# One kernel for attention and two mixtures of experts: attention units in pairs, first-mixture blocks of 256 tokens, and three weights at another start in SBUF

## The chip, the cores and the metric

The kernel runs on one core of a Trainium2 chip. The metric is device time in microseconds (us) of one execution. Before the change, three timed runs gave 1914.37, 1915.16 and 1915.44 us (median 1915.16).

## The reference, cut to what matters

Three stages follow one another; the output of one is the input of the next.

```python
def attention(r, k, v, w, u):             # each (4, 8, 768, 48), u (8, 48)
    for t in range(768):                  # per batch and head, state is 48 x 48
        y[t]  = r[t] @ (state + outer(u * k[t], v[t]))
        state = w[t][:, None] * state + outer(k[t], v[t])

def first_mixture(x, w1, w2, w3, w_out):  # x (3072, 384), w1, w2 (384, 1024)
    return ((x @ w1) * (x @ w2)) @ w3 @ w_out

def second_mixture(x, w_gate, w1, w2):    # 8 experts, w1[e] (384, 1024), w2[e] (1024, 384)
    P = exp(logits - logits.max()),  logits = x @ w_gate
    for _ in range(8):                    # Sinkhorn
        P /= P.sum(1); P /= P.sum(0); P *= N / E
    return sum(P[:, e:e+1] * (relu(x @ w1[e]) @ w2[e]) for e in range(8))
```

## The kernel before, in words

**Stages.** The program has three parts. The first (to about 131 us) is written out by hand in a list, `START`: it loads and splits the weights of the first mixture, multiplies w3 by w_out into one weight W34 (384 columns), runs attention units 0 to 6 and starts the first mixture. The second (131 to 437 us) is the loop over slots at line 800, which weaves attention units 7 to 23 and the rest of the first mixture together. The third (437 us to the end) is the second mixture, with expert weights streamed in, TensorE products `zp` (256 columns) and `yp` (384 columns), and the Sinkhorn steps in between. The change rewrites the second part; of the first and third the order of work stays almost as it was.

**Attention.** A unit is 128 tokens of one batch, all heads. For each unit, VectorE runs two scans over the decay w (`scan_f` line 277, `scan_g` line 281) and makes scaled K and R (`ks`, `rp`); GpSimd makes `rk`, the cross factors `kx` and `rx`, and the diagonal term `ec`. TensorE then has small products of 64 by 64: `sc` (K against R, line 325), `trn` (a transpose of K), `yt1` (masked scores times v, into the PSUM tiles `yt`), `up` (K times v, the state's increment) and `yt2` (R times the state, added into `yt`). VectorE folds `up` into the state in eight instructions a unit (`sn_`, line 378), and ScalarE copies `yt` into the block's `xraw`.

**First mixture.** Tokens go through in 8 blocks of 384 (`BLK`), three units each. `x_high` and `x_low` split x into two parts for TensorE (`xhl`); each weight is split the same way (W1 into `w1h`, `w1l` and so on), and a product takes three matmuls: high by high, high by low, low by high. For each of 8 slices f of the hidden width, `pa` (x by W1) and `pb` (x by W2) take 9 matmuls each; ScalarE moves `pa` out (`asb`), VectorE multiplies (`gs`), ScalarE and GpSimd split the product (`gh`, `gl`). `moe_x2` (line 507) takes g by W34 into `po`, 72 matmuls a block. So a block has 8 x 2 x 9 + 72 = 216 matmuls whose moving side is as wide as the block. `moe_log` (line 528) makes the logits of a group of tokens: step 0 multiplies by the gate (`pl`) and VectorE copies that to `lt`; step 1 transposes `lt` on TensorE (`plt`) and VectorE copies that to `L`. One group is one block.

**What sets the order.** Each engine runs its instructions in the order the program issues them. In the loop, four slots make a unit: phase 0 queues the next unit's preparation in `aux`, of which one or two steps are taken in each slot; phase 1 issues `yt2` of the unit before, then `sc` and `trn`; phase 2 issues `yt1`, `up` and the state; phase 3 issues `yt2` once in three units. A slot further carries one `pa`/`pb` pair or a quarter of `po`, by the table `slices`; `logs` places the two steps of the logits one slot apart; the pre-sums of x for the second mixture (`x2s`, `pre_x`) come from the lists `PLACES` and `LASTPLACES`. A stretch in which TensorE leaves the wide matmuls for the small products and comes back is called a visit below.

Of the kernel before, what the change touches and what calls it, by code (L numbers as in the profile page):

```python
# [22 lines left out]
LAG = 3  # L23
LOG0 = 1
S0 = 28
# [36 lines left out]
def tile_rwkv_moe_sinkhorn_moe(  # L62
# [21 lines left out]
    P = 128  # L84
# [6 lines left out]
    BLK = 384  # L91
    UB = BLK // P
    NB = NT // BLK
# [4 lines left out]
    T = 256  # L98
# [19 lines left out]
    mask = const.tile([P, DP], F32, name="mask")  # L118
    eye = const.tile([P, DP], F32, name="eye")
# [5 lines left out]
    lt = const.tile([GP * UB, P], F32, name="lt")  # L125
    nc.vector.memset(gate, 0.0)
    L = const.tile([P, NTT, E], F32, name="L")

# [25 lines left out]

# [17 lines left out]
    w34l = moe.tile([P, NF, DM], F32R, name="w34l")  # L172
    wo = moe.tile([P, NF, DM], F32, tag="gh", name="wo")
# [119 lines left out]
    def ks(n):  # L293
        st[n]["K"] = t = att.tile([P, 34 * 32], F32, tag="K", bufs=1, name="Kt")
        gv = st[n]["G"][:, 1:529].rearrange("p (c b s) -> p b c s", b=2, s=33)[:, :, :, 1:33]
        (nc.gpsimd if n in KS_POOL else nc.vector).tensor_tensor(diag(t), nat["k", n % 2].rearrange("p (a b s) -> p b a s", b=2, s=32), gv, op=ALU.mult)

    def rp(n):
        st[n]["R"] = t = att.tile([P, 34 * 32], F32, tag="R", bufs=2, name="Rt")
        (nc.gpsimd if n in RP_POOL else nc.vector).tensor_tensor(off(t)[:, ::-1], nat["r", n % 2].rearrange("p (a b s) -> p b a s", b=2, s=32),  # L300
                                tot(n)[:, :, :, 0:32], op=ALU.mult)

    def kx(n):
        t = st[n]["K"]
        for g, m_ in enumerate((st[n]["M"][:, 1, :], tot(n)[:, 1, :, 32])):
            nc.gpsimd.tensor_tensor(off(t)[:, g], diag(t)[:, 1 - g], m_.unsqueeze(2).to_broadcast([P, 8, 32]),
                                    op=ALU.mult)

    def rx(n):
        t = st[n]["R"]  # L310
        for g, m_ in enumerate((st[n]["M"][:, 0, :], tot(n)[:, 0, :, 32])):
            nc.gpsimd.tensor_tensor(diag(t)[:, g], off(t)[:, 1 - g], m_.unsqueeze(2).to_broadcast([P, 8, 32]),
                                    op=ALU.mult)
# [11 lines left out]
    def sc(n):  # L325
        Rt, Kt = st[n]["R"], st[n]["K"]
        st[n]["sc"] = s_ = [psa.tile([P, NP, DP], F32, tag=f"sc{h}", name=f"sc{h}") for h in range(2)]
        for p in range(NP):
            for c in range(2):
                for h in range(2):  # L330
                    cs = slice((4 * p + 2 * c) * 32, (4 * p + 2 * c + 2) * 32)
                    mm(s_[h][64 * c:64 * c + 64, p, :], Kt[64 * h:64 * h + 64, cs], Rt[64 * h:64 * h + 64, cs],
                       True, True, pos=(64 * h, 64 * c))

    def trn(n):
        if n - 1 in st:
# [18 lines left out]
    def yt1(n):  # L355
        d = st[n]
        A, vt = d["A"], nat["v", n % 2].rearrange("p (h d) -> p h d", d=DP)
        d["yp"] = yp = [psa.tile([P, NP, DP], F32, tag=f"yt{c}", name=f"yt{c}") for c in range(2)]
        for p in range(NP):
            for h in range(2):  # L360
                for c in range(2):
                    rs = slice(64 * c, 64 * c + 64)
                    o = 64 * (h if c else 1 - h)
                    mm(yp[c][o:o + 64, p, :], vt[rs, 2 * p + h, :], A[rs, h, p, :],
                       p == 0, n % UPB == 0 and c == 0 and p == NP - 1, pos=(64 * c, o))

    def up_(n):
        d = st[n]
        vt = nat["v", n % 2].rearrange("p (h d) -> p h d", d=DP)
        d["up"] = up = [psa.tile([P, NP, DP], F32, tag=f"sc{c}", name=f"up{c}") for c in range(2)]  # L370
        for p in range(NP):
            for h in range(2):
                for c in range(2):
                    rs = slice(64 * c, 64 * c + 64)
                    mm(up[c][64 * h:64 * h + 64, p, :], d["kn"][rs, p, 64 * h:64 * h + 64], vt[rs, 2 * p + h, :],
                       True, True, pos=(64 * c, 64 * h))

    def sn_(n):
# [3 lines left out]
        for c in range(2):  # L382
            sn = att.tile([P, NP, DP], F32, tag="S", bufs=3, name="Sn")
# [12 lines left out]
    def yt2(n):  # L396
        yp, ss, Rt = st[n]["yp"], st[n]["ss"], st[n]["R"]
        for p in range(NP):
            for h in range(2):
                for c in (1, 0):  # L400
# [4 lines left out]
                    cs = slice((16 + 4 * p + 2 * c) * 32, (18 + 4 * p + 2 * c) * 32)  # L405
                    mm(yp[c][o:o + 64, p, :], ss[c][rs, p, :], Rt[rs, cs], False, p == NP - 1, pos=(64 * h, o))

    def xraw(n):
        yp = st.pop(n)["yp"]
        blk, q = n // UB, n % UB  # L410
        if q == 0:
            xr[blk] = moe.tile([P, NP, BLK], F32, tag="xraw", name="xraw")
        xt = xr[blk]
        nc.scalar.activation(xt[:, :, q * P + 64:q * P + 128], yp[1], AF.Copy)
        for h in range(2):
            nc.scalar.activation(xt[64 * h:64 * h + 64, :, q * P:q * P + 64], yp[0][64 - 64 * h:128 - 64 * h], AF.Copy)

    def xd_(n):
        blk, q = n // UB, n % UB
        xt = xr[blk]  # L420
        if blk == NB - 1 or q == UB - 1:
            ts_ = slice(q * P, (q + 1) * P) if blk == NB - 1 else slice(0, BLK)
            for j in range(KD):
                for h in range(2):
                    nc.sync.dma_start(xt[64 * h + D:64 * h + 64, j, ts_],
                                      xt[64 * h + DQ * j:64 * h + DQ * (j + 1), NP - 1, ts_])

    def stage_a0(n):
        rk(n)
        aux.extend([lambda f=f: f(n) for f in (scan_f, scan_g, small, ks, rp, kx, rx)] + [lambda: (cc(n), ec(n))])  # L430

    def each(n, *fs):
        for f in fs:
            f(n)
# [3 lines left out]
    def x_high(blk, q=None):  # L438
        xt = xr[blk]
        if blk not in xs:  # L440
            xhl = moe.tile([P, 2, KD, BLK], F32R, tag="xhl", name="xhl")
            xs[blk] = (xhl[:, 0], xhl[:, 1])
        xh, xl = xs[blk]
        ts_ = slice(0, BLK) if q is None else slice(q * P, (q + 1) * P)
        nc.scalar.activation(xh[:, :, ts_], xt[:, 0:KD, ts_], AF.Copy)

    def x_low(blk, q=None):
        xt = xr[blk]
        xh, xl = xs[blk]
        ts_ = slice(0, BLK) if q is None else slice(q * P, (q + 1) * P)  # L450
        nc.vector.tensor_tensor(xl[:, :, ts_], xt[:, 0:KD, ts_], xh[:, :, ts_].bitcast(F32), op=ALU.subtract)
# [5 lines left out]
    def ab(blk, f, nm, wh, wl):  # L457
        xh, xl = xs[blk]
        m_t[nm, blk, f] = pt = ps.tile([P, BLK], F32, tag={"pa": "mA", "pb": "mB"}[nm], bufs=2, name=nm)
# [800 lines left out]
```

## Time and profile before

| quantity | value |
|---|---|
| timed runs | 1914.37, 1915.16, 1915.44 us |
| the profiled execution | 1915.92 us, span 1914.2 us |
| TensorE busy in the span | 1888.8 us (99%) |
| VectorE, ScalarE, GpSimd busy | 1378.7 us (72%), 686.2 us (36%), 650.0 us (34%) |
| granted TensorE clock | 1.00 |

Read it so: TensorE is busy from about 131 us on without a break, so a change is worth what it takes off or adds to TensorE's own stream, including waits that it opens there. The other engines matter only through the waits they cause. Busy times of TensorE count a matmul longer than the distance to the next one, since matmuls overlap; the distance from start to start is the cost.

### The profile page before, as it was taken

How to read it: one execution, taken by the hardware profiler on the slowest of the kernel's cores; microseconds unless marked ns; L12 is line 12 of the kernel's file. 1: busy time of each engine (PE TensorE's matmuls, PEld its weight loads, DVE VectorE, ACT ScalarE, POOL GpSimd, SP SyncE). 2: the span in 40 equal slices, each digit the busy share in tenths (PEclk: the TensorE clock that was granted, in tenths of full speed). 3: DMA queues.
4: the chain of work that ended last, by engine and by line, in shares of the span. 5: the costliest groups of instructions: out<-in, count | busy, mean ns of one | idle time of the engine just before them, and what ended most of it. 6: DMA issues, size and time to landing. Idle time of an engine off the chain costs nothing.

```text
span 1914.2 us, 38103 instructions
## 1 busy us (share of the span) xinstructions
PE 1888.8 (99%) x15499; PEld 1842.9 (96%) x15499; DVE 1378.7 (72%) x2409; ACT 686.2 (36%) x1322; POOL 650.0 (34%) x867
## 2 busy tenths in 40 slices
PE   6999999999999999999999999999999999999999
PEld 3799999999999999999999999999999999999999
DVE  8866777765887887676767677667677777667666
ACT  6733333344333333333333333333333333333322
POOL 6766666635431313122222222222323231322200
PEclk9999999999999999999999999999999999999999
DMA  9622444346655555555555555555555555555463
GB/s 379 230 87 91 140 134 140 105 148 239 235 184 191 190 196 197 182 199 183 202 188 197 185 200 187 193 176 208 175 200 185 197 194 193 191 182 188 173 204 121
DMA packets 90494, 353.76 MB, mean 185 GB/s; under 512 B 10384, under 2 KB 34256, under 8 KB 64592
## 3 DMA queue, kind: packets, MB, share of 16 engines
q1 hardware_dynamic: 90320, 351.34, 53.1%
q8 instruction: 122, 2.00, 0.4%
q14 instruction: 52, 0.43, 0.1%
HBM read 329.67 MB, written 20.45 MB: 183 GB/s over the span
## 4 chain that ended last, share of the span: by engine, by line
PE 94%; DMA 2%; DVE 2%; ACT 1%; issue 0%; SPq 0%; DVEq 0%; ACTq 0%
PE yp L114 41%; PE zp L114 34%; PE po L114 5%; PE pa L114 5%; PE pb L114 5%; DMA raw<-in_moe_w_dram 1%; PE yt L114 1%; PE w34ps L114 1%; PE trn L114 1%; DMA nat_kn<-in_kn_dram 1%; PE sc L114 1%; PE up L114 0%; PE pl L114 0%; DVE cvp L229 0%; DVE Sn L388 0%
## 5 line engine op out<-in xcount | busy, mean ns | idle before, releaser
L114 PE MATMUL zp<-xc,w1c 128*128 128x256 f32 x5760 | 793.7, 277 | 1.0 <-DVE ct L915 0.6
L114 PEld LDWEIGHTS zp<-xc,w1c 128*128 128x128 f32 x5760 | 766.7, 188 | 4.8 <-ACT ct L922 1.3
L114 PE MATMUL yp<-w2h,hl 128*128 128x384 f32 x1536 | 515.0, 335 | 0.6 <-DVE hl L912 0.6
L114 PE MATMUL yp<-w2l,hh 128*128 128x384 f32 x1536 | 514.6, 335 | 0.0
L114 PE MATMUL yp<-w2h,hh 128*128 128x384 f32 x1536 | 513.1, 334 | 0.0
L907 ACT ACTIVATE hh<-ct 128x512 fp32r<-128x512 f32 x384 | 236.8, 632 | 526.3 <-DVE ct L915 265.8
L915 DVE TENSOR_TENSOR ct<-ct,zp 128x512 f32<-128x512 f32 x576 | 377.3, 681 | 47.0 <-PE zp L114 41.4
L620 POOL TENSOR_TENSOR w1c<-w1s,w1c 128x512 fp32r<-128x512 f32 (+1 forms) x120 | 127.6, 1064 | 779.9 <-ACT w1c L616 779.9
L922 ACT ACTIVATE ct<-zp 128x512 f32<-128x512 f32 x256 | 153.6, 600 | 440.8 <-PE zp L114 440.8
L114 PEld LDWEIGHTS yp<-w2h,hl 128*128 128x128 f32 x1536 | 288.3, 188 | 1.0 <-DVE hl L912 0.9
L114 PEld LDWEIGHTS yp<-w2h,hh 128*128 128x128 f32 x1536 | 288.4, 188 | 0.2 <-issue 0.2
L114 PEld LDWEIGHTS yp<-w2l,hh 128*128 128x128 f32 x1536 | 288.4, 188 | 0.0
L1087 DVE SCALAR_TENSOR_TENSOR acc<-yp,Pm,acc 128x384 f32<-128x384 f32 x336 | 205.8, 613 | 103.9 <-PE yp L114 103.8
L912 DVE SCALAR_TENSOR_TENSOR hl<-ct,hh 128x512 fp32r<-128x512 f32 x384 | 276.5, 734 | 0.0
L918 DVE TENSOR_TENSOR ct<-ct,zp 128x512 f32<-128x512 f32 x128 | 87.9, 687 | 162.8 <-PE zp L114 162.8
L918 DVE TENSOR_TENSOR ct<-zp,ct 128x512 f32<-128x512 f32 x128 | 88.3, 690 | 74.6 <-ACT ct L922 62.7
L620 POOL TENSOR_TENSOR w1c<-w1raw,w1c 128x128 fp32r<-128x128 f32 (+1 forms) x90 | 56.7, 630 | 195.3 <-ACT w1c L616 195.3
L612 POOL TENSOR_TENSOR w1s<-w1raw 128x128 f32<-128x128 f32 x240 | 120.8, 524 | 0.2
L487 POOL TENSOR_TENSOR gl<-gs,gh 128x384 fp32r<-128x384 f32 x64 | 75.4, 1179 | 104.0 <-ACT gh L483 101.2
L114 PE MATMUL pa<-xhl,w1h 128*128 128x384 f32 x384 | 100.4, 342 | 1.5 <-ACT w34s L255 1.5
L114 PE MATMUL pb<-xhl,w2h 128*128 128x384 f32 x384 | 98.1, 336 | 0.4 <-DVE cv L230 0.4
L478 DVE TENSOR_TENSOR gs<-pb,asb 128x384 f32<-128x384 f32 x64 | 35.4, 553 | 66.6 <-PE pb L114 48.1
(130 smaller groups left out, 1908.6 us busy)
## 6 DMA issues: line engine op xcount, KB each, us to landing
xc<-xd SPq DMA_DIRECT2D x192, 1024.0 KB, 4.9
xc<-xd SPq DMA_DIRECT2D x64, 768.0 KB, 4.3
xd<-x2s SPq DMA_DIRECT2D x53, 256.0 KB, 2.7
w1raw<-in_e_w_dram SPq DMA_DIRECT2D x32, 384.0 KB, 3.1
w2raw<-in_e_w_dram SPq DMA_DIRECT2D x32, 384.0 KB, 3.1
raw<-in_moe_w_dram SPq DMA_DIRECT2D x8, 1024.0 KB, 9.5
nat_w<-in_w_dram SPq DMA_DIRECT2D x24, 264.5 KB, 3.4
nat_k<-in_kt_dram SPq DMA_DIRECT2D x24, 256.0 KB, 4.0
```

Source lines behind the costliest of these rows:

```text
L114: nc.tensor.matmul(o, lhsT, rhs, start=start, stop=stop, **kw)
L478: nc.vector.tensor_tensor(t, m_t.pop(("pb", blk, f)), m_t.pop(("asb", blk, f)), op=ALU.mult)
L487: nc.gpsimd.tensor_tensor(gl[:, f, :], m_t.pop(("gs", blk, f)), gh[:, f, :].bitcast(F32), op=ALU.subtract)
L612: eng.tensor_tensor(tmp_[:, many.index(r), :], at_(a), at_(b), op=ALU.add if sg == 1 else ALU.subtract)
L620: eng.tensor_tensor(lo[:, d0:d1, :], sv, hi[:, d0:d1, :].bitcast(F32), op=ALU.subtract)
L907: nc.scalar.activation(hh, src, AF.Relu)
L912: nc.vector.scalar_tensor_tensor(hl, src, 0.0, hh.bitcast(F32), op0=ALU.max, op1=ALU.subtract)
L915: nc.vector.tensor_tensor(o, a, b_, op=ALU.add)
L918: nc.vector.tensor_tensor(o, a, b_, op=ALU.subtract)
L922: nc.scalar.activation(t, src, AF.Copy)
L1087: nc.vector.scalar_tensor_tensor(dst, yp, so["Pm"][:, tt, e:e + 1], dst, op0=ALU.mult, op1=ALU.add)
```

## The change

Five things change, all in the second part of the program.

1. **Blocks.** The first two blocks keep 384 tokens; the other 2304 tokens go in nine blocks of 256 in place of six of 384 (`BLKS`). A group of logits is four tiles of 128 tokens (six groups) in place of three (eight groups).
2. **Pairs.** From unit 7 on, two units go together through `sc`, `trn`, `yt1`, `up`, the state and `yt2`. A chunk c has 24 steps: eight of `po` for block c+1, then 16 of `pa` and `pb` for block c+2. A `turn` before step 0 has `yt2` of the old pair, `sc` and `trn` of the new one; a `middle` before step 9 has `yt1`, `up` and the states of a pair.
3. **A table of times.** `aux`, `slices` and `logs` are replaced by hooks at 24*c + j. The logits stand at steps 8.6 and 9.6 of chunks 0, 1, 3, 5 and 7; the sixth group comes later, in the second mixture.
4. **Buffers.** K and R of a unit live in halves of one tile `krr` with rings of spare places, and from unit 10 on the loads of r, k, w, rn and kn have one buffer each (v keeps two). `pre_group` goes; all pre-sums are `pre_x` pieces, and part of the first expert weights is prepared on GpSimd.
5. **Starts in SBUF.** Small gap tiles are put in so that `w1h`, `w1l`, `w2h`, `w2l`, `w34h` and `w34l` begin at 160 modulo 256 bytes of a partition. Before, all six begin at 96. The moving tiles `xhl`, `gh` and `gl` begin at 96 in both kernels.

```diff
-    BLK = 384
-    NB = NT // BLK
+    T = 256
+    BLKS = [(0, 384), (384, 384)] + [(t, T) for t in range(768, NT, T)]
+    NB = len(BLKS)
+    FU = 6
+    NC = NB - 2
...
+    const.tile([P, 16], F32, name="gap_const")
+    mw.tile([P, 16], F32, name="gap_mw")
     w1h = mw.tile([P, KD, FF], F32R, name="w1h")
...
     w34l = moe.tile([P, NF, DM], F32R, name="w34l")
+    moe.tile([P, 48], F32, name="gap_moe")
...
-    def sc(n):
+    def sc(*us):
+        s_ = pair("sc")
+        for u_, n in enumerate(us):
...
-    def yt1(n):
+    def yt1(*us):
+        yp = pair("yt")
...
-    def up_(n):
+    def up_(*us):
+        up = pair("sc")
...
-    def moe_log(blk, step, pool=None, tag="mA", bufs=2):
+    UL = P // GP
+    def moe_log(grp, step, pool=None, tag="mA", bufs=2):
...
+    def prep(n, base, scale=1.0):
+        def put(d, *fs):
+            event(base + 0.5 + d * scale, *fs)
+        put(0, lambda: rk(n), lambda: scan_f(n))
+        put(1, lambda: scan_g(n))
...
+        put(6, lambda: rx(n))
+        put(8.8, lambda: cc(n))
+        put(9.6, lambda: ec(n))
...
+    def middle(*us):
+        yt1(*us)
+        up_(*us)
+        for n in us:
+            sn_(n)
...
-    for s in range(S0, NSL):
...
+    for k in range(NC):
+        step(k, -0.5, lambda k=k: turn(k, k + 1))
+        step(k, 4.6, lambda k=k: x_high(k + 2))
+        step(k, 5.6, lambda k=k: x_low(k + 2))
+        if k + 1 < NC:
+            step(k, 9 - 0.5, lambda k=k: middle(*units(k + 1)))
+        if k + 2 < NC:
+            n = FU + 2 * k + 4
+            prep(n, 24 * k + 1)
+            prep(n + 1, 24 * k + 12)
...
+    step(0, 8.6, lambda: moe_log(0, 0))
+    step(0, 9.6, lambda: moe_log(0, 1))
+    for g_ in range(1, NTT // UL - 1):
+        step(2 * g_ - 1, 8.6, lambda g_=g_: moe_log(g_, 0))
+        step(2 * g_ - 1, 9.6, lambda g_=g_: moe_log(g_, 1))
...
+    for c in range(-1, NC):
+        for j in range(10 if c < 0 else 0, 24):
+            run(24 * c + j)
+            if j < 8:
+                moe_x2(c + 1, j, 8)
+            else:
+                f = (j - 8) // 2
+                if j % 2 == 0:
+                    pa(c + 2, f)
...
+                else:
+                    pb(c + 2, f)
...
```

The order of instructions shows where the logits stand. First TensorE in the slot loop of the kernel before, at one of the eight groups of logits: the end of a `pb`, the product `pl`, and then a visit; the transpose `plt` comes 46 rows on.

```order
L114 MATMUL pb<-xhl,w2h 128x384 x2
L114 MATMUL pb<-xhl,w2l 128x384
L114 MATMUL pl<-x2s,gate 32x128 x9
L114 MATMUL yt_3642<-Rt,Sn 64x64
L114 MATMUL yt_3641<-Rt,Sn 64x64
```

The transpose itself stands before the next visit's first product:

```order
L114 MATMUL pb<-xhl,w2h 128x384 x2
L114 MATMUL pb<-xhl,w2l 128x384
L114 MATMUL plt<-ident,lt 128x96
L114 MATMUL yt_3887<-ec,nat_v_103 64x64
L114 MATMUL yt_3888<-ec,nat_v_103 64x64
```

So between the two stand a visit and two products `pa`, `pb` of nine wide matmuls each. TensorE after the change, chunk 3: the last two rows of the pair's `up` (its PSUM tiles have the tag `sc`, its left operands are `krr` and `nat_v`), `pl`, one `pb`, `plt`, and the next `pa`.

```order
L113 MATMUL sc_3874<-nat_v_105,krr 64x64
L113 MATMUL sc_3875<-nat_v_105,krr 64x64
L113 MATMUL pl<-x2s,gate 32x128 x12
L113 MATMUL pb<-xhl,w2h 128x256 x2
L113 MATMUL pb<-xhl,w2l 128x256
L113 MATMUL pb<-xhl,w2h 128x256 x2
L113 MATMUL pb<-xhl,w2l 128x256
L113 MATMUL pb<-xhl,w2h 128x256 x2
L113 MATMUL pb<-xhl,w2l 128x256
L113 MATMUL plt<-ident,lt 128x128
L113 MATMUL pa<-xhl,w1h 128x256 x2
L113 MATMUL pa<-xhl,w1l 128x256
```

Now `pl` follows the pair's `up` at once, and only one `pb` of nine stands between `pl` and `plt`. VectorE before, around the copy to `lt` that `plt` needs:

```order
L478 TENSOR_TENSOR gs<-pb,asb 128x384
L283 SCALAR_TENSOR_TENSOR Gt<-nat_w_106,d_63 128x527
L538 COPY lt<-pl 96x128
L350 COPY_PREDICATED ec<-mask,sc_3819 128x256
L350 COPY_PREDICATED ec<-mask,sc_3820 128x256
```

VectorE after, at the same group of chunk 3 (`Sn` with its 64-column pieces is the state; the last four go to a spare place in `nat_n1`):

```order
L766 TENSOR_TENSOR x2s<-x2s 128x256
L509 TENSOR_TENSOR xhl<-xraw,xhl 128x768
L456 SCALAR_TENSOR_TENSOR Sn<-s_more,T_3226,sc_3874 128x64 x4
L456 SCALAR_TENSOR_TENSOR Sn<-Sn,T_3226,sc_3875 128x64 x4
L456 SCALAR_TENSOR_TENSOR Sn<-Sn,T_3486,sc_3874 128x64 x4
L456 SCALAR_TENSOR_TENSOR nat_n_110<-Sn,T_3486,sc_3875 128x64 x4
L598 COPY lt<-pl 128x128
L536 TENSOR_TENSOR gs<-pb,asb 128x256
L602 COPY L<-plt 128x32
```

The copy to `lt` stood behind a scan and ahead of the mask copies; it now stands behind all sixteen instructions of the pair's state.

## Rows read from the trace of the kernel before

**Rows 1.** The page: TensorE's busy time, and the chain's shares by line.

```profile
PE 1888.8 (99%) x15499; PEld 1842.9 (96%) x15499; DVE 1378.7 (72%) x2409; ACT 686.2 (36%) x1322; POOL 650.0 (34%) x867
PE yp L114 41%; PE zp L114 34%; PE po L114 5%; PE pa L114 5%; PE pb L114 5%; DMA raw<-in_moe_w_dram 1%; PE yt L114 1%; PE w34ps L114 1%; PE trn L114 1%; DMA nat_kn<-in_kn_dram 1%; PE sc L114 1%; PE up L114 0%; PE pl L114 0%; DVE cvp L229 0%; DVE Sn L388 0%
```

**Rows 2.** Second part: window, us, busy PE, PEld, DVE, ACT, POOL, clock, DMA, GB/s.

```profile
131.00:437.00 306.00, 306.00 (x3771) 291.86 (x3767) 216.65 (x470) 119.16 (x278) 180.87 (x167) 1.00 0.39 122
```

**Rows 3.** TensorE's timeline at two visits (start us, us, then the group).

```profile
371.98 0.34 PE L114 MATMUL pb<-xhl,w2l 128*128 128x384 f32 x1
372.25 0.86 PE L114 MATMUL pl<-x2s,gate 128*32 128x128 f32 x18
373.04 0.69 PE L114 MATMUL yt<-Rt,Sn 64*64 64x64 f32 x32
...
374.54 0.59 PE L114 MATMUL pa<-xhl,w1h 128*128 128x384 f32 x2
374.98 0.34 PE L114 MATMUL pa<-xhl,w1l 128*128 128x384 f32 x1
...
377.76 0.25 PE L114 MATMUL plt<-ident,lt 96*128 96x96 f32 x1
...
379.02 0.62 PE L114 MATMUL pa<-xhl,w1h 128*128 128x384 f32 x2
379.48 0.35 PE L114 MATMUL pa<-xhl,w1l 128*128 128x384 f32 x1
...
380.72 0.51 PE L114 MATMUL pb<-xhl,w2h 128*128 128x384 f32 x2
...
382.28 0.51 PE L114 MATMUL pa<-xhl,w1h 128*128 128x384 f32 x2
```

**Rows 4.** The same view in the second mixture: 256-wide products in the steady stream.

```profile
543.46 1.53 PE L114 MATMUL zp<-xc,w1c 128*128 128x256 f32 x12
544.82 0.33 PE L114 MATMUL yp<-w2h,hh 128*128 128x384 f32 x1
```

**Rows 5.** The same view where the second mixture begins.

```profile
453.97 0.87 PE L114 MATMUL zp<-xc,w1c 128*128 128x256 f32 x6
454.68 0.34 PE L114 MATMUL po<-gl,w34h 128*128 128x384 f32 x1
```

**Rows 6.** The same view again, the first matmul after a visit.

```profile
203.85 0.62 PE L114 MATMUL pa<-xhl,w1h 128*128 128x384 f32 x2
```

**Rows 7.** VectorE's timeline: the unit's state after that visit, and a scan.

```profile
204.03 1.61 DVE L388 SCALAR_TENSOR_TENSOR Sn<-Sn,T,up 128x64 f32<-128x64 f32 x8
205.57 0.68 DVE L300 TENSOR_TENSOR Rt<-nat_r,Ft 128x512 f32<-128x512 f32 x1
...
212.56 2.09 DVE L279 TENSOR_TENSOR_SCAN Ft<-nat_w,d 128x528 f32<-128x528 f32 x1 [1.23 <-POOL Rt L312]
```

**Rows 8.** VectorE's timeline beside the visits of rows 3.

```profile
370.57 1.25 DVE L279 TENSOR_TENSOR_SCAN Ft<-nat_w,d 128x528 f32<-128x528 f32 x1
...
374.67 0.26 DVE L538 COPY lt<-pl 96x128 f32<-96x128 f32 x1
374.85 0.77 DVE L350 COPY_PREDICATED ec<-mask,sc 128x256 f32<-128x256 uint32 x2
```

**Rows 9.** VectorE's groups from 131 to 437 us (count, busy us, mean ns).

```profile
L283 DVE TENSOR_TENSOR_SCAN Gt<-nat_w,d 128x527 f32<-128x527 f32 x16 | 28.3, 1769 | 0.0
L279 DVE TENSOR_TENSOR_SCAN Ft<-nat_w,d 128x528 f32<-128x528 f32 x15 | 27.0, 1800 | 8.7 <-POOL Rt L312 8.7
...
L699 DVE TENSOR_TENSOR x2s<-x2s 128x256 f32<-128x256 f32 x34 | 24.8, 732 | 0.4
L706 DVE TENSOR_TENSOR x2s<-x2s 128x256 fp32r<-128x256 f32 x38 | 14.1, 419 | 1.1 <-ACT x2s L703 1.1
L350 DVE COPY_PREDICATED ec<-mask,sc 128x256 f32<-128x256 uint32 x34 | 12.9, 433 | 0.0
L296 DVE TENSOR_TENSOR Kt<-nat_k,Gt 128x512 f32<-128x512 f32 x16 | 12.1, 758 | 0.0
```

More of the change, by code (lines that the diff above doesn't have):

```diff
@@ new lines, in ks @@
+        if n < FU + 3:
+            t = krr[:, 0:34 * 32]
+            st[n]["K"] = both(t)
+            eng.tensor_tensor(diag(t), kv, gv, op=ALU.mult)
+            if n == FU + 2:
+                ka_home.extend([both(t)[0], nat["w", 1][:, 0:HALF]])
+                kk_ring.extend([st[n - 1]["kn"].rearrange("p a b -> p (a b)"), both(t)[1], nat_n1[:, 0:HALF]])
+                kk_ring.rotate(-2)
+        else:
+            st[n]["K"] = K = ka_home[n % 2], kk_next()
+            for g in range(2):
+                eng.tensor_tensor(alt(K[g], g), kv[:, g], gv[:, g], op=ALU.mult)
@@ L423, in xd_ @@
+    def xd_(n):
+        blk, q = UBLK[n]
+        xt = xr[blk]
+        if (q + 1) * P == BLKS[blk][1]:
             for j in range(KD):
                 for h in range(2):
[L425 to L434, printed above, removed]
@@ L436, in tile_rwkv_moe_sinkhorn_moe @@
-    xs = {}
[L438 to L442, printed above, removed]
-        xh, xl = xs[blk]
[L444 to L451, printed above, removed]
+                    nc.sync.dma_start(xt[64 * h + D:64 * h + 64, j, :],
+                                      xt[64 * h + DQ * j:64 * h + DQ * (j + 1), NP - 1, :])
@@ L711, in pre_x @@
         return sums, high, low
-    def pre_group(sb, g, tag, tmp_, eng):
-        t = spaced(pools["w"], [P, 2, len(XP_[g][4]), T], F32R, tag, "xpre")
-        sums, high, low = factors(XP_, g, XB, x2[sb], tmp_, t, eng)
-        def end():
-            low()
-            xd[sb, g] = dram.tile(list(t.shape), F32, name=f"xd{sb}{g}")
-            nc.sync.dma_start(xd[sb, g], t.bitcast(F32))
-        return sums, high, end
     def ld_x(n, g):
@@ L776, in tile_rwkv_moe_sinkhorn_moe @@
[L776 to L786 removed]
+        return [lambda i=i: part(i) for i in range(3)]
@@ new lines, in prep @@
+    def prep(n, base, scale=1.0):
[3 more added lines that the diff above has]
+        put(1, lambda: scan_g(n))
+        put(2, lambda: small(n))
+        put(3, lambda: ks(n))
+        put(4, lambda: rp(n))
+        put(5, lambda: kx(n))
+        put(6, lambda: rx(n))
+        put(8.8, lambda: cc(n))
+        put(9.6, lambda: ec(n))
+        for nm, d in (("rn", 2), ("kn", 2), ("w", 4), ("k", 6), ("r", 7)):
+            m = n + (2 if n < ONE - 1 else 1)
+            if m < NU and not n == ONE - 1 - 0:
+                put(d, lambda nm=nm, m=m: load(m, (nm,)))
@@ L787, in tile_rwkv_moe_sinkhorn_moe, with front, front_end @@
+    def front(*us):
+        sc(*us)
+        for n in us:
+            trn(n)
+    def front_end(*us):
+        for n in us:
+            kn_(n)
+        for n in us:
+            cp_(n)
+    def middle(*us):
+        yt1(*us)
+        up_(*us)
+        for n in us:
+            sn_(n)
     tx0 = []
@@ new lines, in tile_rwkv_moe_sinkhorn_moe, with units, turn @@
+    s_more = att.tile([P, NP, DP], F32, name="s_more")
+    def units(k):
+        return tuple(u_ for u_ in (FU + 2 * k, FU + 2 * k + 1) if u_ > FU)
+    def turn(k_old, k_new):
+        old, new = (units(k) if 0 <= k <= NC - 1 else () for k in (k_old, k_new))
+        for n in old:
+            yt2(n)
+        if new:
+            front(*new)
+        if old:
+            xraw(*old)
+            xd_(old[-1])
+        if new:
+            front_end(*new)
+    step(-1, 10 - 0.5, lambda: turn(-1, 0))
@@ new lines, in tile_rwkv_moe_sinkhorn_moe @@
+    for sb_ in range(NS - 1):
+        for m_, r_ in enumerate(ORDER):
+            if sb_ < NS - 2:
+                t_, w_, d_ = 24 * 3 * sb_ + 9.7 + 4.2 * m_, WORK[m_ % 4], (5, 9)
+            elif m_ < 3:
+                t_, w_, d_ = 24 * 3 * sb_ + 9.7 + 4 * m_, WORK[(0, 1, 3)[m_]], (4, 8)
+            else:
+                t_, w_, d_ = 24 * (3 * sb_ + 1) + 1.7 + 1.75 * (m_ - 3), LATE[m_ % 6], (2, 4)
+            place(t_, *d_, lazy(lambda sb_=sb_, r_=r_, w_=w_: pre_x(sb_, r_, w_(), 0, nc.vector)))
@@ new lines, in open_w @@
+    def open_w():
+        st_attn.close()
+        pools["w"] = ctx.enter_context(tc.tile_pool(name="wp", bufs=1, side="right", reuse_waits="tile"))
+        ld_w1(0)
+        ld_w1(1)
+        st_pa.close()
+        pools["z"] = ctx.enter_context(tc.tile_pool(name="psz", bufs=1, space=PSUM, side="right",
+                                                    reuse_waits="tile"))
+        for g in range(2):
+            spaced(pools["w"], [P, 4, T], F32, f"w1c{g}0", "unused")
+            ld_x(0, g)
@@ L1143, in sk_both @@
         sk_rows()
-    for x_ in late:
-        sk.append(lambda x_=x_: moe_log(*x_, pool=pools["y"], tag="col", bufs=1))
+    for t_ in range(2):
+        sk.append(lambda t_=t_: moe_log(NTT // UL - 1, t_, pool=pools["y"], tag="col", bufs=1))
     sk.extend([sk_max0, sk_max1, sk_max2])
```

383 lines of the change are left out of this document (178 added, 205 removed).

## The prediction

> **What bounds the kernel now.** I read the page's busy shares and its chain of waits first. TensorE is busy 99% of the span, and five of its products (`yp`, `zp`, `po`, `pa`, `pb`) hold 90% of the chain [rows 1]. Then the windows: from 131 to 437 us, the part that the change rewrites, TensorE is busy 306.00 us of 306.00 at a granted clock of 1.00, while VectorE is busy 216.65 us (71%), GpSimd 59% and ScalarE 39% [rows 2]. No wait of TensorE is left there to take away. So the change can gain only by making TensorE's stream cheaper, and any wait that it opens is lost in full. The last view is TensorE's timeline, for the distance from one matmul's start to the next; the busy time counts overlaps twice and is no use for that.
>
> **The wide matmuls.** In both kernels the first two blocks have 384 tokens. The other 2304 tokens cost 6 blocks of 216 = 1296 matmuls before, and 9 of 216 = 1944 after. Before, nine matmuls of 384 columns take from 380.72 to 382.28, so 173.3 ns each [rows 3], and 1296 x 173.3 = 224.6 us. A 256-wide product in a like shape exists in the second mixture: twelve `zp` take 543.46 to 544.82, 113.3 ns each [rows 4]. At the start of that mixture six take 453.97 to 454.68, 118.3 ns each [rows 5]. With these, 1944 cost 220.3 us (-4.3) or 230.0 us (+5.4). I take 113.7, near rows 4, because that is how a 256-wide product runs in a steady stream, and the second part is one; the few in rows 5 stand at the end of a long run of 384-wide `po`. That is 221.0 us, a gain of 3.6.
>
> The new starts of the weights I cost at nothing beside this. No row shows what a start is worth: the `zp` of rows 4 and those of rows 5 read the same kind of tiles at the same starts, 160 for the weight and 96 for the moving side, yet differ by 5 ns. If the start decides for `pa`, `pb` and `po`, its worth lies between these two rows, so within the ends already named.
>
> The Trainium skill ("TensorE: Matmul & The Clock Gate", Back-to-back issue gap) gives the gap of an isolated matmul at full clock as its columns over 2.4 ns plus 2.5 ns. By it 384 columns cost 162.5 ns and 256 cost 109.2, and the blocks' sum would go from 210.6 to 212.3 us, 1.7 slower in place of 3.6 faster. Both rows lie above it, by 10.8 and 4.1 ns, so the excess is no constant here, and I go by the rows.
>
> **The visits.** Each time TensorE leaves the wide stream for small products and comes back, it loses something at either edge. Entering: from the start of the last `pb` to `pl` is 371.98 to 372.25, 0.27 in place of 0.173, so 0.10. Leaving: two `pa` take 374.54 to 374.98, 0.44 in place of 0.347, and 379.02 to 379.48, 0.46; so 0.09 and 0.11 [rows 3]. A visit costs about 0.21 us. From 131 us to the first `zp` I count 41 visits in the order before and 19 after: 22 x 0.21 = 4.6 us gained. The small products themselves stay the same in number, and so does the gate's: 8 x 9 small `pl` before, 6 x 12 after.
>
> **The new wait.** `plt` needs the copy of `pl` to `lt`. Before, `pl` starts at 372.25, the copy is over by 374.85 [rows 8], and `plt` comes at 377.76 [rows 3], so 2.9 us are to spare. After, `pl` follows the pair's `up` directly, only one `pb` stands between it and `plt`, and on VectorE the copy stands behind the pair's sixteen state instructions. Call the end of `up` T. A visit ends at 203.85 [rows 6] and the state starts at 204.03; eight of its instructions take until 205.57, 0.193 each [rows 7]. So sixteen run from T + 0.18 to T + 3.26, and with the copy's 0.26 [rows 8] `plt` may start at about T + 3.5. TensorE is there sooner: `pl` has 24 passes at 0.79 / 18 [rows 3] = 1.05, `pb` 9 x 0.1137 = 1.02, with the edge 0.2, so T + 2.3. It waits 1.25 us. Behind `plt` on TensorE stands all that follows, the next `pa` first, so nothing covers it. The group occurs in chunks 0, 1, 3, 5 and 7: 5 x 1.25 = 6.3 us lost. Bounds: nothing, if the state of the first unit starts while the second unit's `up` still runs and the copy is early; 5 x 3 = 15 if VectorE is itself 1.75 us late with the state.
>
> **VectorE's load.** Per pair it has 2 x (1.80 + 1.77 for scans, 0.76 and 0.68 for K and R, 0.76 for mask copies, 1.54 for the state) = 14.6 us [rows 7, 9]. A chunk adds eight `gs` at about 0.42 (the two-input 256-wide sum, 419 ns [rows 9]) = 3.4, `x_low` at about 0.9, and 24 / 4.2 = 5.7 pieces of the second mixture's sums at (24.8 + 14.1) / 38 = 1.02, so 5.8. With a microsecond for small ones that is 26 us. TensorE's chunk is 216 x 0.1137 = 24.6 and 2 x 2.6 of small products (1.50 from 373.04 to 374.54, 1.1 within 377.76 to 379.02 [rows 3]), with edges and gate some 30.8. So VectorE is about 84% busy in chunks 0 to 6, against 71% before, and its work comes in lumps: two scans and a sum can stand ahead of something TensorE wants. Bounds: 0, if each lump lies where TensorE is far from it, and 14 us, by the third rival. I take 2 in all, nearer to 0, because `gs`, `x_low` and the states stand in the table where their inputs become ready.
>
> At nothing I cost the rest: the single buffers for r, k, w, rn and kn (a chunk of 30 us lies between a pair's loads and their use; if that cover goes, a load's few us appear once a unit in a scan's start), the rings for K and R, the copy of whole pairs by ScalarE (39% busy), and GpSimd's share of the expert weights. The second mixture keeps its order; the first `zp` just starts when the second part ends.
>
> **Sum.** 1915.92 - 3.6 - 4.6 + 6.3 + 2 = 1916.0 for an execution like the profiled one. The median of the runs shown lies 0.76 lower, so 1915.3; call it 1915.5.
>
> **Rivals.**
> - B, the waits stay hidden: VectorE starts the states with the first unit's `up`, or `gs` and the copy find it free, and only the two gains are left: 1915.16 - 8.2 = 1907. For it: VectorE still idles a sixth of the chunk. Against it: sixteen instructions in a row are sixteen, and 3.1 us exceed the 2.1 us of `pl` and `pb`.
> - C, VectorE cannot follow in the seven heavy chunks. The trace has the same scan at 1.25 us and at 2.09 [rows 7, 8]; with the pair's factors crowded the long form rules, 4 scans a pair add 4 x 0.3 = 1.2 us to the 26, and a lump of 2 us lies ahead of `x_low`. `x_low` is issued at step 5.6 and the block's first `pa` at step 8, so about 2.4 x 1.02 = 2.4 us later; less its own 0.9, it decides from 1.5 us of backlog on. Then TensorE waits about 2 us a chunk, 7 x 2 = 14 in place of 2: 1927. For it: 84% is an average, and the logits add to it. Against: TensorE's own stalls give VectorE time back.
> - D, what a matmul costs above its columns does not shrink with its width, and the changed starts do not alter that. The 384-wide rows lie 13.3 ns above 160.0, the 256-wide of rows 4 lie 6.6 above 106.7 and those of rows 5 11.6. At 118.3 ns the wide sum is 9.0 more than I took: 1924.5. The Trainium skill's rule above has such a constant, though a smaller one. For it: rows 5 stand right beside `po`, whose neighbours they would be. Against: `zp` in the long stream keeps 113.3. This is also the case in which the new starts do nothing that the change could be after.
>
> **How the numbers follow.** This kernel's runs can tell about 0.2%, 3.8 us, from no change. My forecast A (gains and new waits cancel) has 0.40, with its own range 1911.5 to 1919.5; B 0.29, C 0.18, D 0.13. Nearly all of A lies within 0.2%: 0.34, with 0.03 to either side. So faster 0.32, same 0.34, slower 0.34. The range runs from 1906.5, which holds B but for its low edge, to 1925, which holds D and leaves out the larger half of C: about 0.16 is left out.
>
> **What would show it.** In the changed kernel's trace: 256-wide `pa` and `pb` 113 to 114 ns apart in mid-slot (D: 118 or more); nineteen visits; five idle times of TensorE ahead of `plt`, some 1.2 us each, released by VectorE's `lt` (B: none); idle times ahead of the first `pa` of a block released by `xhl`, few (C: seven of 2 us); and the first `zp` within 2 us of where it is now. I am wrong if TensorE shows waits for loads or for GpSimd's factors ahead of `sc`, which I cost at nothing, or if the second mixture itself changes its length.

## The result, and the profile after

The changed kernel takes 1932.13 us (median of 5 runs, 1931.54 to 1934.70) against 1915.16: a ratio of 1.0092, 95% interval [1.0077, 1.0107], so about 17 us slower. The forecast was no change, and the time lies above its range. The span of the profiled execution is 1933.0 us, 18.8 more than before. The profiled executions of starts_96, plt_late and starts_224 below have `zp` 115.5 ns apart in the second mixture in place of 114.1, some 8 us in all, so of these three only the second part is read.

The window that answers to [rows 2] (same columns) shows where: TensorE had no idle time in it before, and has now.

```profile
131.00:437.00 306.00, 289.60 (x4236) 280.80 (x4228) 227.89 (x485) 108.23 (x271) 171.89 (x184) 0.99 0.36 110
```

TensorE's waits from 131 to 520 us in the changed kernel (who waits, for what; us in total, times, the longest). Before, the same view held only the last two kinds and one `yp` wait of 0.6 us.

```profile
PE plt L113 <- DVE lt L598: 7.2, 5, 2.0
PE pb L113 <- DVE gs L536: 6.2, 8, 1.3
PE pa L113 <- DVE xhl L509: 2.9, 6, 0.6
PE yp L113 <- DVE hl L993: 2.2, 1, 2.2
PE zp L113 <- ACT ct L1003: 1.2, 1, 1.2
PE pl L113 <- issue: 0.7, 1, 0.7
PE zp L113 <- DVE ct L996: 0.6, 1, 0.6
PE zp L113 <- DVE ct L999: 0.3, 1, 0.3
```

All three large ones have VectorE at the other end. The second mixture as a whole did not grow. These rows of the two kernels give the first and last start of its `zp` (min, median and max ns, then the starts in us): it begins 19.6 us later and lasts 1458.4 us where it lasted 1459.7. First before, then after:

```profile
L114 PE MATMUL zp<-xc,w1c x5760: 276/276/387, 437.2 to 1896.9; 128*128 128x256 f32 x199
```

```profile
L113 PE MATMUL zp<-xc,w1c x5760: 276/276/394, 456.8 to 1915.2; 128*128 128x256 f32 x199
```

One part of the 18.8 us is no wait. In chunk 5, behind its longest wait for `plt`, TensorE runs at a granted clock of 0.50 (1.2 GHz) from 345.8 to 349.2 us, and nine `pb` take 1.92 us there, 213 ns each. The windows row first (columns of [rows 2]), then TensorE's timeline:

```profile
346.00:349.00 3.00, 3.00 (x16) 3.00 (x16) 0.40 (x2) 0.38 (x1) 0.43 (x1) 0.50 0.90 244
```

```profile
344.92 0.30 PE L113 MATMUL plt<-ident,lt 128*128 128x128 f32 x1 [1.98 <-DVE lt L598]
...
346.38 0.63 PE L113 MATMUL pb<-xhl,w2h 128*128 128x256 f32 x2
...
348.30 0.63 PE L113 MATMUL pa<-xhl,w1h 128*128 128x256 f32 x2
```

That stretch costs 1.6 us against the usual distance. The kernel before has a granted clock of 1.00 in the whole second part [rows 2]. Of the five timed executions two have a mean clock of 0.999 (1934.70, the profiled one, and 1933.33 us) and three 1.000 (1931.54, 1931.80 and 1932.13), so the median's 17 us stand without such a stretch.

The wait ahead of `plt`, TensorE's timeline in chunk 0, which answers to [rows 3]:

```profile
173.59 0.86 PE L113 MATMUL pl<-x2s,gate 128*32 128x128 f32 x24
174.38 0.50 PE L113 MATMUL pb<-xhl,w2h 128*128 128x256 f32 x2
...
177.23 0.30 PE L113 MATMUL plt<-ident,lt 128*128 128x128 f32 x1 [1.53 <-DVE lt L598]
```

And VectorE beside it, the first and last of the state's four groups, then the copy, which answers to [rows 7, 8]:

```profile
173.73 0.86 DVE L456 SCALAR_TENSOR_TENSOR nat_n<-Sn,T,sc 128x64 f32<-128x64 f32 x4 [7.15 <-PE sc L113]
...
176.04 0.85 DVE L456 SCALAR_TENSOR_TENSOR Sn<-Sn,T,sc 128x64 f32<-128x64 f32 x4
176.80 0.28 DVE L598 COPY lt<-pl 128x128 f32<-128x128 f32 x1
```

`pl` follows `up` at 173.59, so that is T; the state takes 173.73 to 176.89, and `plt` starts at T + 3.6; the forecast had T + 3.5.

The waits for `gs` are the other kind. VectorE in chunk 2, without a gap:

```profile
246.69 1.79 DVE L302 TENSOR_TENSOR_SCAN Ft<-nat_w,d 128x528 f32<-128x528 f32 x1
248.41 1.20 DVE L766 TENSOR_TENSOR x2s<-x2s 128x256 fp32r<-128x256 f32 x1
249.53 0.41 DVE L536 TENSOR_TENSOR gs<-pb,asb 128x256 f32<-128x256 f32 x1
249.87 1.72 DVE L306 TENSOR_TENSOR_SCAN Gt<-nat_w,d 128x527 f32<-128x527 f32 x1
251.50 0.22 DVE L313 RECIPROCAL Mt<-Ft 128x16 f32<-128x16 f32 x1
251.65 0.77 DVE L314 TENSOR_TENSOR T<-Ft 128x8 f32<-128x8 f32 x1
252.34 0.41 DVE L536 TENSOR_TENSOR gs<-pb,asb 128x256 f32<-128x256 f32 x1
```

From `gs` to `gs` is 2.8 us, and TensorE's pair `pa`, `pb` takes 18 x 0.1133 = 2.04. `pb` has two PSUM buffers, so VectorE may be one slot late and not two. Further on in the same lump TensorE stands still:

```profile
254.87 0.28 PE L113 MATMUL pa<-xhl,w1l 128*128 128x256 f32 x1
256.43 0.50 PE L113 MATMUL pb<-xhl,w2h 128*128 128x256 f32 x2 [1.29 <-DVE gs L536]
```

The step from start to start is 1.56 us in place of 0.113: the wait costs 1.45, not the 1.29 that the view calls idle, and the step behind it (0.23 us) is another 0.11 longer than usual.

The distance of the wide products, TensorE's timeline at two places, which answers to [rows 4, 5]. First `pa` and the next `pb` in the middle of a chunk, then a `po` run from its second matmul to the `pa` behind it:

```profile
242.13 0.39 PE L113 MATMUL pa<-xhl,w1h 128*128 128x256 f32 x2
...
243.15 0.39 PE L113 MATMUL pb<-xhl,w2h 128*128 128x256 f32 x2
```

```profile
228.63 0.28 PE L113 MATMUL po<-gl,w34h 128*128 128x256 f32 x1
...
236.99 0.28 PE L113 MATMUL pa<-xhl,w1h 128*128 128x256 f32 x1
```

Nine in 1.02 us are 113.3 ns each; 71 `po` in 8.36 us are 117.7. Nearly every `po` (501 of 568), and under half of `pa` and `pb`, run at the slower distance. Over the 1776 undisturbed 256-wide steps ahead of the first `zp` the mean is 115.9 ns.

### The profile page after: what moved, and what is told of

Its sections match the earlier page's. It is cut to its first block, busy times and chain, and to the rows that moved or that the text cites. A ratio compares the mean times of both kernels' runs of the same rounds, so it can differ in the third digit from the quotient of the medians.

```text
span 1933.0 us, 39529 instructions
## 1 busy us (share of the span) xinstructions
PE 1886.9 (98%) x16145; PEld 1846.2 (96%) x16145; DVE 1401.3 (72%) x2452; ACT 684.2 (35%) x1342; POOL 651.8 (34%) x903
## 4 chain that ended last, share of the span: by engine, by line
PE 75%; DVE 1%; ACT 0%; issue 0%; POOL 0%; DVEq 0%; ACTq 0%
PE yp L113 41%; PE zp L113 34%; PE po L113 0%; DVE ct L996 0%; DVE hl L993 0%; DVE acc L1164 0%; ACT hh L988 0%; ACT ct L1003 0%; ACT gh L541 0%; PE pcs L113 0%; DVE w2l L740 0%; PE pl L113 0%; POOL gl L545 0%; ACT w2h L739 0%; DVE ct L999 0%
## 5 line engine op out<-in xcount | busy, mean ns | idle before, releaser
L545 POOL TENSOR_TENSOR gl<-gs,gh 128x256 fp32r<-128x256 f32 (+1 forms) x88 | 76.0, 869 | 126.4 <-ACT gh L541 126.4
L113 PE MATMUL pb<-xhl,w2h 128*128 128x256 f32 (+1 forms) x528 | 106.3, 296 | 6.7 <-DVE gs L536 6.2
L113 PE MATMUL pa<-xhl,w1h 128*128 128x256 f32 (+1 forms) x528 | 105.9, 293 | 3.7 <-DVE xhl L509 2.9
L113 PEld LDWEIGHTS pb<-xhl,w2h 128*128 128x128 f32 x528 | 83.2, 190 | 10.6 <-DVE gs L536 8.5
```

The lines of the kernel that those rows point to most:

```text
L113: nc.tensor.matmul(o, lhsT, rhs, start=start, stop=stop, **kw)
L545: nc.gpsimd.tensor_tensor(gl[:, f, :], m_t.pop(("gs", blk, f)), gh[:, f, :].bitcast(F32), op=ALU.subtract)
```

## Experiments

Each kernel was timed beside the kernel before on the same chip, and the ratios are to that. Theory W: the time is lost in TensorE's waits for VectorE. Rival S: the 256-wide products are dear, and the new starts decide it. Under W there is a second question, whether VectorE has too much to do (load) or only the wrong thing next (order).

**starts_96.**

```diff
-    const.tile([P, 16], F32, name="gap_const")
...
-    mw.tile([P, 16], F32, name="gap_mw")
     w1h = mw.tile([P, KD, FF], F32R, name="w1h")
...
     w2l = mw.tile([P, KD, FF], F32R, name="w2l")
+    mw.tile([P, 16], F32, name="gap_mw")
...
-    moe.tile([P, 48], F32, name="gap_moe")
+    moe.tile([P, 64], F32, name="gap_moe")
...
-        m2.tile([P, 112], F32, name="gap_m2")
+        m2.tile([P, 128], F32, name="gap_m2")
```

> The changed kernel with w1h, w1l, w2h, w2l, w34h and w34l at 96 modulo 256 again; nothing else moves by a byte. Theory W (the loss is waits that TensorE now has for VectorE, the starts are worth nothing): 1932 us, within 2. Theory S (the 256-wide matmuls are what is dear, and their spacing hangs on the starts): pa and pb leave 113 ns and go to 118 or more throughout, some 1000 matmuls by 5 ns or more, so 1937 us or above; or, if 160 is the worse start, po falls from 118 to 113 ns, 500 by 5 ns, and 1929.5.

Measured: 1935.23 us, ratio 1.0112 [1.0095, 1.0130], between the two forecasts. In its second part 4 of 1788 256-wide steps kept 113 to 115 ns (782 of 1776 in the changed kernel); the mean excess over 113.5 was 6.3 ns (11.3 us in all, against 4.2 in the changed kernel). So S is right that the starts set the distance. But the waits shrank as the products grew, those for `gs` from 6.2 to 3.6 us and those for `xhl` from 2.9 to 1.2, so 7 us of slower products cost only 3, which this pair of runs can't tell from none.

**plt_late.**

```diff
-    step(0, 9.6, lambda: moe_log(0, 1))
+    step(0, 12.6, lambda: moe_log(0, 1))
-        step(2 * g_ - 1, 9.6, lambda g_=g_: moe_log(g_, 1))
+        step(2 * g_ - 1, 12.6, lambda g_=g_: moe_log(g_, 1))
```

> The changed kernel with the transpose plt three steps later (step 12.6 in place of 9.6). Theory W: the five idle times ahead of plt, 7.2 us in the profile, go, and with each some 0.27 us of getting back to speed, so 1923.5 us within 2. Rival V (VectorE is behind anyway, and the time comes back as waits for gs or xhl): 1929 to 1932.

Measured: 1926.10 us, ratio 1.0062 [1.0049, 1.0076]: 6 us less than the changed kernel, and between the two forecasts. TensorE's waits up to 450 us:

```profile
PE pb L113 <- DVE gs L536: 7.1, 9, 1.3
PE pa L113 <- DVE xhl L509: 2.8, 5, 0.9
PE pl L113 <- issue: 1.4, 1, 1.4
```

The kind `plt` is gone; `gs` has taken 0.9 us of it.

**half_scans.**

```diff
-        nc.vector.tensor_tensor_scan(t, src("w", n)[:, 0:528], d1[:, 0:528], 0.0, op0=ALU.mult, op1=ALU.add)
...
+        c_ = 528 if n < FU + 4 else 264
+        nc.vector.tensor_tensor_scan(t[:, 0:c_], src("w", n)[:, 0:c_], d1[:, 0:c_], 0.0, op0=ALU.mult, op1=ALU.add)
...
```

> The changed kernel, but from unit 10 on the two scans cover only half of their columns (the other half keeps what an earlier unit left), so each scan is about 0.8 us shorter; all else stands where it stood. Theory V (VectorE's load delays gs and xhl): the waits for gs (6.2 us) and xhl (2.9 us) shrink to 2 or less in sum and 1921 to 1925 us results, with the waits ahead of plt still there at 5 to 7 us. Rival P (it is the places in the table and not the load): the waits stay and 1931 us or more results.

Measured: 1925.26 us, ratio 1.0051 [1.0038, 1.0064]. Its waits:

```profile
PE plt L113 <- DVE lt L606: 7.5, 5, 2.0
PE pb L113 <- DVE gs L544: 2.5, 3, 1.3
...
PE pa L113 <- DVE xhl L517: 0.6, 1, 0.6
```

The `gs` and `xhl` kinds fell from 9.1 to 3.1 us and `plt` kept its own, near what theory V forecast. So the scans are most of what delays them; shorter scans are less load and smaller lumps at once, and this run does not part the two.

**before_160.** The kernel before with the gaps (mask and eye moved to the pool of the attention to make room).

> The kernel before, with only the starts of the six weights moved from 96 to 160 modulo 256 (mask and eye change pool to make room, the moving tiles stay at 96). Theory W: 1915 us within 2, 384-wide matmuls 173 to 174 ns apart as before. Theory S: their spacing changes by some ns; 1300 matmuls by 5 ns would give 1908.5 or 1921.5.

Measured: 1916.32 us, ratio 1.0007 [0.9998, 1.0015]. The starts alone gain nothing where the products are 384 wide. In its trace these stand 174.9 ns apart on average, against 173.7 before, and the first `zp` comes 1.6 us later; the ratio can't tell that from no change.

**fix_low.** On top of plt_late:

```diff
-        step(k, 5.6, lambda k=k: x_low(k + 2))
+        step(k, 4.9, lambda k=k: x_low(k + 2))
```

> The later plt of plt_late, and x_low issued at step 4.9 in place of 5.6, ahead of the first unit's R on VectorE (its input from ScalarE was there 1.4 us before VectorE came to it). If each wait ahead of a block's first pa is only this order: the waits for xhl (2.8 us, 0.27 more each) go and 1926.1 becomes about 1922. Rival V (VectorE is short of time, the wait comes back at gs): 1925 or more.

Measured: 1922.19 us, ratio 1.0036 [1.0023, 1.0048], as forecast. Waits up to 437 us:

```profile
PE pb L113 <- DVE gs L536: 6.0, 8, 1.3
PE pa L113 <- DVE xhl L509: 0.5, 2, 0.2
```

**fix_g.** On top of fix_low, the second unit's steps behind its first scan come one step later:

```diff
-    def prep(n, base, scale=1.0):
+    def prep(n, base, scale=1.0, more=0):
...
-            event(base + 0.5 + d * scale, *fs)
+            event(base + 0.5 + d * scale + (more if d else 0), *fs)
...
-            prep(n + 1, 24 * k + 12)
+            prep(n + 1, 24 * k + 12, 1.0, 1)
```

> As fix_low, and the second unit's preparation behind its first scan one step later, so that its two scans no longer stand in three steps with the gs of the same slots. If the lump of scans is what delays gs: the waits for gs (7.1 us in nine) shrink to some 3 and about 1918 us results. If the total load delays gs: no change against fix_low, within 1.5 us. A third outcome: the factors come too late for the next pair's sc, slower than fix_low.

Measured: 1915.51 us, ratio 1.0001 [0.9992, 1.0010]. Its one kind of wait up to 437 us, and VectorE at the lump shown above:

```profile
PE pb L113 <- DVE gs L536: 2.7, 3, 1.2
```

```profile
243.24 1.79 DVE L302 TENSOR_TENSOR_SCAN Ft<-nat_w,d 128x528 f32<-128x528 f32 x1
244.96 1.20 DVE L766 TENSOR_TENSOR x2s<-x2s 128x256 fp32r<-128x256 f32 x1
246.08 0.41 DVE L536 TENSOR_TENSOR gs<-pb,asb 128x256 f32<-128x256 f32 x1
246.42 1.72 DVE L306 TENSOR_TENSOR_SCAN Gt<-nat_w,d 128x527 f32<-128x527 f32 x1
248.06 0.39 DVE L536 TENSOR_TENSOR gs<-pb,asb 128x256 f32<-128x256 f32 x1
```

The work is the same, instruction for instruction, and from 131 to 437 us VectorE is busy 234.8 us where it was 235.0 in fix_low; the next `gs` now comes right behind the second scan, 1.98 us after the one before. So order alone can take more than half of these waits away (6.0 to 2.7 us of idle time): 6.7 us less than fix_low, for one step. Some 5 of them remain where the mean clock is alike, 1.000, since fix_low's two such runs took 1920.73 and 1920.86 us and the median of fix_g's eight is 1915.6. The edit also moves K, R and what GpSimd makes of them by the step; what each of these gave was not tested.

**fix_pool.** On top of fix_low:

```diff
-            place(t_, *d_, lazy(lambda sb_=sb_, r_=r_, w_=w_: pre_x(sb_, r_, w_(), 0, nc.vector)))
+            place(t_, *d_, lazy(lambda sb_=sb_, r_=r_, w_=w_, m_=m_: pre_x(sb_, r_, w_(), 0, nc.gpsimd if m_ % 3 == 1 else nc.vector)))
```

> As fix_low, and every third piece of the second mixture's sums (about 2 us a chunk) runs on GpSimd in place of VectorE. If VectorE's load delays gs: the waits for gs shrink to some 3 us and about 1918 us results. Rival: GpSimd's work beside VectorE makes VectorE's scans as much longer, or makes gl late, and it is no faster than fix_low.

Measured: 1924.13 us, ratio 1.0048 [1.0035, 1.0061]; the waits for `gs` are 6.8 us in six, one of 2.5. That is no gain, but it doesn't speak against load, since VectorE's load hardly fell. These are the windows of fix_low and of fix_pool (columns of [rows 2]):

```profile
131.00:437.00 306.00, 299.43 (x4324) 292.06 (x4319) 235.01 (x510) 113.06 (x286) 172.54 (x190) 1.00 0.39 120
```

```profile
131.00:437.00 306.00, 298.21 (x4308) 291.04 (x4307) 232.98 (x477) 112.39 (x283) 201.91 (x218) 0.99 0.39 120
```

The sums that stay on VectorE are 14.7 us less, yet it is busy only 2.0 us less, because much of what stays grew, such as the second scan (1.62 to 1.84 us on average) and R (0.57 to 0.72), beside a GpSimd that is busy 29 us more. This is the rival that the expectation named.

**fix_g_96, moving_160, starts_224.** On top of fix_g, the starts alone: weights back at 96; weights at 160 and the moving tiles at 160 too; weights at 224.

> fix_g with the six weights back at 96 modulo 256, as starts_96 was to the changed kernel. If a start is worth what the spacing in starts_96 showed (every 256-wide product of the second part at about 120 ns, none at 113) and waits had swallowed half of it: 5 to 6 us above fix_g, 1920.5 to 1921.5, with spacings of 118 to 121 throughout. If the starts are worth only the 3 us that starts_96 lost: 1918.5. If that profile was a chance: 1915.5.

> fix_g with the moving tiles of the first mixture (xhl, gh, gl) at 160 modulo 256 too, the weights staying at 160. If what matters is that weight and moving side differ by 64: all 256-wide products at 118 to 120 ns as with both at 96, so 5 us above fix_g, 1920.5. If only the weight's own start matters: 1915.5 and the same mixture of 113 and 118 ns.

> fix_g with the six weights at 224 modulo 256, so 128 from the moving tiles in place of 64. If a larger distance frees po as well, which at a distance of 64 stays at 118 ns in nearly all its 576 products: up to 1181 products by 4.4 ns, 5 us less than fix_g, 1910.5. If any distance other than 0 does the same: 1915.5 and the same mixture of 113 and 118. If 64 is the one good distance: 118 to 121 throughout, as in fix_g_96, 1919 to 1920.

Measured: 1919.16 us, ratio 1.0020 [1.0012, 1.0029]; 1919.95, 1.0022 [1.0013, 1.0031]; and 1927.87, 1.0020 [1.0011, 1.0029] on a chip on which the kernel before took 1923.93. The first two stand clear of fix_g's 1.0001 [0.9992, 1.0010]: 3.7 to 4.4 us, between the forecasts of 3 and of 5 us or more. By its trace fix_g_96 loses 6.8 us on the 256-wide products, gains 0.5 on the 384-wide ones, and 1.7 of the waits that fix_g has left are gone. TensorE's timeline of fix_g_96 in mid-chunk:

```profile
240.58 0.40 PE L113 MATMUL pa<-xhl,w1h 128*128 128x256 f32 x2
...
241.66 0.40 PE L113 MATMUL pb<-xhl,w2h 128*128 128x256 f32 x2
```

Nine take 1.08 us, 120 ns each, and moving_160 has the same 120. So it is no property of 160: with weight and moving side both at 96 or both at 160 at most 4 of 1822 steps keep 113 to 115 ns. Nor is it the chip: fix_k below, at 160 against 96 on the same chip, has 722 of 1812. A distance of 128 was no better than 64, as far as the slower chip lets one say: 263 of its 1820 steps took 112 to 115 ns, the others 116 to 126, which is nearest to the third outcome.

**fix_k.** On top of fix_g, the second unit's K and R one step later still.

> fix_g with the second unit's K and R (and what GpSimd makes of them) another step later, since two of the three waits that fix_g has left (1.2 us each) stand ahead of a gs that VectorE does behind K and a sum. If it is again the order: those two go and 1913 us results. If the load decides, they move to the next gs: 1915 to 1916. If the factors then miss the next pair's sc: slower than fix_g.

Measured: 1917.64 us, ratio 1.0008 [0.9999, 1.0017]. By its waits it is the third outcome, though in time it isn't clear of fix_g. The margin is used up on both sides now:

```profile
PE sc L113 <- POOL krr L358: 1.7, 4, 0.4
PE pb L113 <- DVE gs L536: 1.4, 4, 0.5
```

No version beat the kernel before; fix_g equals it.

## Why the prediction was wrong

The terms of the sum, against what the two traces give when TensorE's starts are followed from 131 us to the end (us, against before):

| step | predicted | measured |
|---|---|---|
| wide matmuls | -3.6 | +0.6 (1944 at 115.9 ns for 1296 at 173.7: +0.2; 198 still 384 wide at 176.0: +0.5) |
| edges of the visits | -4.6 | -5.1 |
| the small products themselves | 0 | -4.2 |
| wait ahead of `plt` | +6.3 | +8.1 (7.2 idle in five, the rest around it) |
| VectorE late otherwise | +2 | +11.9 (6.2 for `gs`, 2.9 for `xhl`, the rest around it) |
| the slower step behind each of these | 0 | +1.7 |
| the stretch at 1.2 GHz | 0 | +1.6 |
| one wait ahead of `pl`, cause not shown | 0 | +0.9 |
| the second mixture's start | 0 | +3.3 |
| sum | 0.1 | +18.8 |

**The step that failed** is VectorE's load: what VectorE would be late apart from `plt`. I worked out VectorE's share of a chunk (84%; measured 79% in chunks 0 to 6, where it is busy 189.2 us of the 240 from 156 to 396), named the lumps, bounded them at 0 and 14 us, and took 2, "because `gs`, `x_low` and the states stand in the table where their inputs become ready". They do, but the table sets only the order of issue, and what stands ahead can be long. A `gs` behind a scan of 1.8 us, a piece of a sum at 1.2 and a second scan starts when those are through, and `x_low` stood behind K and R, for which TensorE's `sc` comes only in the next chunk, at 363.7: in chunk 5 ScalarE had its input ready at 334.8, but VectorE came to it 1.4 us later, as the changed kernel's two timelines show (VectorE, then TensorE):

```profile
334.46 0.75 DVE L331 TENSOR_TENSOR krr<-nat_k,Gt 128x256 f32<-128x256 f32 x2
335.14 1.17 DVE L347 TENSOR_TENSOR krr<-nat_r,Ft 128x256 f32<-128x256 f32 x2
336.23 1.38 DVE L509 TENSOR_TENSOR xhl<-xraw,xhl 128x768 fp32r<-128x768 f32 x1
```

```profile
337.67 0.38 PE L113 MATMUL pa<-xhl,w1h 128*128 128x256 f32 x1 [0.54 <-DVE xhl L509]
```

TensorE goes on as `x_low` ends. Rival C had this mechanism with 14 us, at `x_low` alone; that place gave 2.9 us of idle time, and the larger part, 6.2, came at `gs`, which only my own term names; its 11.9 us lie within the bounds of 0 and 14 that I gave it, but not near the 2 that I took. C had 0.18 and not more because I read 84% as slack, where the slack that counts is one slot of 2.04 us.

**The wide matmuls** were the second miss, 4 us. I took the starts as worth nothing beyond the rows, and for the average took rows 4 in place of a mixture. The rows' two distances are both there in the changed kernel, half and half; without the new starts nearly all of it would have been at 120, so the worth of a start did not lie between the rows' 113.3 and 118.3, as I had it. The Trainium skill's rule ("TensorE: Matmul & The Clock Gate", Back-to-back issue gap) gave an estimate of +1.7 for this term, which looks nearer than my -3.6, but not for its reason: it has 109.2 ns at 256 columns, and the traces have 113 to 120. Rival D forecast the slow distance throughout for the case that the starts do nothing; they do something, and only as far as 113 ns is not lost again.

**Right:** the gain at the edges of the visits, and the wait ahead of `plt`, by place, count and length: 1.53, 1.52, 0.68, 1.98 and 1.52 us where 1.25 was worked out from eight state instructions and a copy. No wait for a load or for GpSimd's factors came up in the changed kernel, as forecast. **Put at nothing:** the small products, 4.2 us cheaper in pairs, for a reason that was not tested, and the stretch at 1.2 GHz. **Too small** was the price of any wait: some 0.27 us on top of each idle time, for the step into it and the slower one behind it, with 19 waits about 5 us. **Missed:** the first wait of `yp` for `hl`, 2.2 in place of 0.6 us, and one of `zp` for ScalarE's `ct`, 1.2 us, among what I had costed at nothing in the second mixture; their cause was not tested.

The three orders that the runs changed account for the loss: plt_late 6.0, `x_low` 3.9, the steps behind the second unit's first scan 6.7, together 16.6 of 17 us. That fix_g then stands at 1.0001, where the forecast was no change, is luck and no proof of the sum. The forecast held 6.3 us for `plt`, which fix_g no longer has, so by its own terms fix_g should be some 6 us faster than before. In fix_g's trace the edges and the small products still give 8.5 us, but the wide products cost 1.4 more than before (at 256 columns 116.3 ns, where the forecast had 113.7), the waits that are left and the steps behind them some 4.3, and the second mixture's start about 3.

## What to carry to other kernels

When an engine is full, an engine behind it that is busy 79% of the time has slack only on average: look at the longest run of work that can stand ahead of the instruction the full engine waits for, and hold it against the buffers in between, here one slot of 2 us. Before load is taken off such an engine, change what it does next; one step in a table gave back 5 to 7 us with the same work. If load is moved to a neighbour, look whether the busy time falls with it; here 14.7 us of sums moved took off 2.0. And making the full engine faster by 7 us gave 3 to 4 as long as it only ran into the waits sooner, so measure such a gain with as few of them left as you can.

## What the runs showed of the hardware

The distance of 256-wide products hangs on the starts of both operands in SBUF. With weight and moving tile at the same start modulo 256 (96 and 96, or 160 and 160) nearly every step is 117 to 121 ns, 119.9 on average; with 160 against 96, 113.3 occurs, but does not hold everywhere: in the changed kernel `po` stays at 117.7 for whole runs of 72, and `pa` and `pb` get back to 113 a few steps behind a stall or not until the next one. What decides between the two in one and the same layout stays open.

384-wide products went the other way, and by less. In fix_g_96 and moving_160 they stand 173.4 to 173.6 ns apart, in the changed kernel and fix_g, at 160 against 96, 176.0; before_160 has 174.9 where the kernel before has 173.7. Over the changed kernel's 198 such products that is 0.5 us, over before_160's some 1.6, and no timed run can tell it from nothing.

TensorE's granted clock fell to 0.50 (1.2 GHz) seven times ahead of the end in these traces, each time within a wait of TensorE of 1.9 to 2.4 us or at most 0.9 us behind it: one fall each in the changed kernel, half_scans, fix_low, fix_pool and moving_160, two in starts_96. Eight other waits of 1.9 to 2.5 us had no fall, and what decides stays open.

VectorE's `x_low` at 768 columns took 1.27 us on average, where 0.9 was estimated from narrower ones, and the low part of a sum 0.63 us against 0.42 before [rows 9], one of them 1.20 in the rows above. Of the changed kernel's 39 low parts the 19 with no GpSimd instruction beside them took 0.41 to 0.42 us, and the 13 that lie wholly beside one 0.43 to 1.20. In the kernel before seven lie so and took 0.42, so it is not every GpSimd instruction; which ones do it was not tested.
